# Row 1's attention interleaved earlier with chunk 0's products, and three small reorderings, in a fused windowed-attention and squared-ReLU kernel

## The chip, the cores and the metric

The kernel runs on one core of one Trainium2 chip. A core has five engines that run beside one another and meet through semaphores: TensorE (PE, matmuls and transposes; its weight loads are shown as PEld), VectorE (DVE), ScalarE (ACT), GpSimd (POOL) and SyncE (SP, which here only issues DMAs). The metric is the device time of one execution in microseconds (us), lower is better.

## The reference

Eight batch rows of 576 tokens, each with eight heads of 64 features, go through causal attention. Heads 0 to 3 see the last 32 tokens (sliding), heads 4 to 7 every fourth of the last 128 (dilated). The heads are then laid side by side as 4608 tokens of 512 features and go through two dense products with a squared ReLU between them.

```python
mask_plain = (rel >= 0) & (rel < window)
mask_dil = (rel >= 0) & (rel < window * dilation) & (rel % dilation == 0)
scores = np.where(masks[None, :, :, :], scale * q @ k.T, -1000000000.0)
attn = softmax(scores)
x = (attn @ v).transpose(0, 2, 1, 3).reshape(B * S, H * D)      # 4608 x 512
h = x @ w_in                                                    # 512 -> 2048
g = np.maximum(h, 0.0) ** 2
out = g @ w_out                                                 # 2048 -> 512
```

## The kernel before, in words

Attention works by batch row (0 to 7, 576 tokens), the dense part by chunk (0 to 8, 512 tokens). Since chunk c spans parts of rows c-1 and c, rows run ahead of chunks: while row b is in attention, the dense steps of an earlier chunk (chunk b-1) fill TensorE.

The order is written by hand. Every engine runs its own instructions in the order in which the program emits them. The dense part is a Python generator, and `pump(n)` (L520) emits its next n steps; a step is two matmuls of 128x512 (or four of 128x256). A call of `pump` between two pieces of attention puts dense work between them on TensorE, and with it the ScalarE and VectorE work of those steps on their queues.

A row of attention has these pieces. Rows 0 and 1 turn q and k by TensorE (`t_sliding` L538, `t_dilated` L556); VectorE and ScalarE copy the result to QKTp and QKTd. From row 2 on, VectorE puts the loaded q and k (tile ns) in token order (`by_token` L118, tile nr), SP writes nr to DRAM (dp) and reads it back through transposing DMAs (L229, L233). `attn_scores` (L712) makes four groups of scores, exponentials on ScalarE and masks on VectorE (tile AT). `attn_values` (L728) makes seven groups of values: three sliding (pav), four dilated (paw). After each, VectorE takes a reciprocal and a product (`normalize`, L622), and TensorE turns the result (px, py) for ScalarE to copy into xT, the dense part's input. The scores, values and, in row 1, the transposes share a PSUM pool of two buffers (`papool`).

`mm1_gen` (L318) is a chunk's first product: 16 groups of four matmuls into ph, each followed by a ReLU on ScalarE (rt) and a square on VectorE (g). Chunk 0's second product is `mm2_by_rows_gen` (L488): 32 steps, the first 24 of which leave nothing; its last eight finish the output tiles po of tokens 0 to 127, 128 to 255, and so on, and `store` (L466) copies each to ot on ScalarE. From chunk 2 on, the second product is done by seven half-size products (`mm2_strassen_gen`, L359), whose operands are sums and differences of parts of g (tile gs, `sum_of_g` L335).

Row 1 (L846 to L861): `pump(1000)` emits the whole first product of chunk 0, `pump(3)` six matmuls of its second product, then come the transposes with `pump(2)` after each, the scores with `pump(2)`, and the values with `pump(1)` (two after the first pav). In the middle of the values, after paw of the first dilated group, `then` puts row 2's `by_token` copy on VectorE and its two stores on SP. On SP these stores are followed by the output of chunk 0's first half (L462, after `store` of its second tile), the four transposing DMAs of row 2, the output of the second half, and the v loads of row 2. Row 2's q and k (ns) are loaded from the POOL queue (L822, which emits L112), behind `cast_sliding_v(1)` and the last quarter of w_out.

At the end (L933 to L937), chunk 7's generator is pumped for 20 steps, then ScalarE copies the second half of row 7's dilated values into xT (L695, called through `second_half`), then chunk 7 is finished and chunk 8 follows. The last half product ends in one add of 128x512 (L444) and one 256 KB DMA (L445).

Of the kernel before, what the change touches and what calls it, by code (L numbers as in the profile page):

```python
# [13 lines left out]
P = 128  # L14
# [3 lines left out]
def kernel(  # L18
# [9 lines left out]
    nc = tc.nc  # L28
# [11 lines left out]
    TOKC = 512  # L40
# [40 lines left out]
    HM = DM // 2  # L81
    HF = NFF // 2
    HTOK = TOKC // 2
# [98 lines left out]
    def halo_sliding(b, mp):  # L182
        m0, m1 = max(1, 2 * mp), 2 * mp + 2
        nc.scalar.copy(
            vp[b % 2][0:PADP, m0:m1, :, 0:D], vp[b % 2][P - PADP : P, m0 - 1 : m1 - 1, :, 0:D]
        )
# [78 lines left out]
    for m, w, pad in (  # L265
# [5 lines left out]
            out=lo_[:, 0:w], in0=relf[:, 0:w], scalar1=-pad - 0.5, scalar2=None, op0=ALU.is_gt  # L271
        )
        nc.vector.tensor_scalar(
            out=hi_[:, 0:w], in0=relf[:, 0:w], scalar1=W - pad - 0.5, scalar2=None, op0=ALU.is_lt
# [6 lines left out]
    for r in range(2):  # L281
        nc.vector.tensor_scalar(
            out=vd[r][:, 0, :, :, D],
# [12 lines left out]
    def mm1_half(c, ffc, ph, dmks, parts=None):  # L296
        lo = c * TOKC % XW
        cut = min(TOKC, XW - lo)
        parts = parts or [(0, cut, lo)] + ([(cut, TOKC, 0)] if cut < TOKC else [])
        for dmk in dmks:  # L300
            for t0, t1, x0 in parts:
                nc.tensor.matmul(  # L302
                    ph[:, t0:t1],
                    wi4[ffc // 4][:, dmk, :, ffc % 4],
                    xT[:, dmk, x0 : x0 + t1 - t0],
                    start=(dmk == 0 and t0 == 0),
                    stop=(dmk == NDM - 1),
                    skip_group_check=parts != [(0, TOKC, lo)],
                )
# [3 lines left out]
    def mm1_begin(c, ffc, parts=None):  # L313
        ph = pmool.tile([P, TOKC], FP32, name=f"ph{c}_{ffc}", tag="pm")
        mm1_half(c, ffc, ph, (0, 1), parts)
        return ph

    def mm1_gen(c, g, sums=False, begun=()):  # L318
        for ffc in range(NFF):
            if ffc < len(begun):  # L320
                ph = begun[ffc]
            else:
                ph = mm1_begin(c, ffc)
                yield
            mm1_half(c, ffc, ph, (2, 3), [(T0, TOKC, T0)] if begun and ffc < len(begun) else None)
            rt = osb.tile([P, TOKC], FP16, name=f"rt{c}_{ffc}", tag="rt")
            nc.scalar.activation(rt, ph[:], ACTF.Relu)  # L327
            nc.vector.tensor_mul(g[:, ffc, :], rt, rt)  # L328
            if c == 1 and ffc % 2 == 0:
                next(w_sums)  # L330
            if sums and ffc % 4 == 3 and ffc >= HF:
                sum_of_g(g, ffc - 3, ffc + 1)
            yield

    def sum_of_g(g, f0, f1):  # L335
        k = slice(f0 - HF, f1 - HF)
        nc.vector.tensor_add(gs[0][:, k], g[:, k, HTOK:], g[:, f0:f1, HTOK:])
        nc.vector.tensor_sub(gs[1][:, k], gs[0][:, k], g[:, k, 0:HTOK])
# [20 lines left out]
    def mm2_strassen_gen(c, g):  # L359
        A, Bk, Ck = "abc"  # L360
        banks = {}

        def wq(r, q):
            return lambda k: wo[2 * r + k // 4][:, k % 4, HM * q : HM * (q + 1)]

        def gq(i, r):
            return lambda k, t: g[:, HF * r + k, HTOK * i + P * t : HTOK * i + P * (t + 1)]

        def tq(n):
            return lambda k: wt[n][:, k]  # L370

        def sq(n):
            return lambda k, t: gs[n][:, k, P * t : P * (t + 1)]

        def product(bank, a, b, ts=(0, 1)):
            new = bank not in banks
            if new:
                banks[bank] = pmool.tile([P, 2, HM], FP32, name=f"p{bank}{c}", tag="pm")
            for t in ts:
                for k in range(HF):  # L380
                    nc.tensor.matmul(  # L381
                        banks[bank][:, t],
                        a(k, t),
                        b(k),
                        start=(new and t == 0 and k == 0),
                        stop=(k == HF - 1),
                        skip_group_check=True,
                    )
                    if k % 4 == 3 and (t, k) != (ts[-1], HF - 1):
                        yield  # L390

        def half(i):
            return otp.tile([P, 2, DM], FP32, name=f"o{i}_{c}", tag="ot")

        def take(o, j):
            ot = o[:, :, HM * j : HM * (j + 1)]
            nc.scalar.copy(ot, banks[A])  # L397
            return ot

        def leave(o, i, js):  # L400
            t0 = c * TOKC + HTOK * i
            m = slice(HM * js[0], HM * (js[-1] + 1))
            nc.sync.dma_start(
                out=out[t0 : t0 + HTOK, m].rearrange("(t p) m -> p t m", p=P), in_=o[:, :, m]
            )

        def add(ot, bank):
            nc.vector.tensor_add(ot, banks[bank], ot)  # L408

        last = c == NTOKC - 1  # L410

        nc.vector.tensor_sub(g[:, 0:HF, HTOK:], g[:, 0:HF, 0:HTOK], g[:, 0:HF, HTOK:])
        yield from product(A, gq(0, 0), wq(0, 0))
        upper = half("u")
        o11 = take(upper, 0)
        yield
        yield from product(Ck, gq(0, 1), wq(1, 0))
        add(o11, Ck)
        if last:
            leave(upper, 0, (0,))  # L420
        yield
        yield from product(A, sq(1), tq(1))
        lower = half("v")
        o21 = take(lower, 0)
        nc.vector.tensor_sub(gs[1], g[:, HF:, 0:HTOK], gs[1])
        yield
        yield from product(Bk, gq(1, 0), tq(2), (0,))
        yield
        yield from product(A, sq(0), tq(0))
        o22 = take(lower, 1)  # L430
        yield
        yield from product(Bk, gq(1, 0), tq(2), (1,))
        add(o22, Bk)
        if last:
            leave(lower, 1, (1,))
        yield
        yield from product(A, sq(1), wq(1, 1))
        take(upper, 1)
        leave(upper, 0, (1,) if last else (0, 1))
        while at_end:  # L440
            at_end.pop()()
        yield
        yield from product(Bk, gq(1, 1), tq(3))
        add(o21, Bk)  # L444
        leave(lower, 1, (0,) if last else (0, 1))  # L445
        yield

    def mm2(c, g, po, t, ffc):
# [71 lines left out]
    def pump(n):  # L520
        for _ in range(n):
            while pending:
                try:
                    next(pending[0])
                    break
                except StopIteration:
                    pending.pop(0)
# [184 lines left out]
    def attn_scores(b, gap, less=0, hooks={}):  # L712
        for hp in range(2):
            s_sliding(b, hp)
            if hp in hooks:
                hooks[hp]()
            pump(gap)
        for g in range(2):
            if g and b == 1:
                halo_sliding(b, 0)  # L720
            s_dilated(b, g)
            if 2 + g in hooks:
                hooks[2 + g]()
            if g and b == 2:
                halo_sliding(b, 0)
            pump(gap - less)

    def attn_values(b, gap, wide=False, then=None):  # L728
        xs = x_tiles(b)
        for mp in range(3):  # L730
            av_sliding(b, mp, xs)
            if b < 3:
                if mp < 2:
                    halo_sliding(b, mp + 1)
                else:
                    halo_dilated(b, 0)
            if then and b > 1 and mp == 4 - b:
                then()
            pump(gap + (b == 1 and mp == 0))
        x_sliding(b, 0, xs, wide)  # L740
        if b < 3:
            halo_dilated(b, 2)
        pump(gap)
        av_dilated(b, 0, 0, xs)
        if then and b == 1:
            then()
        pump(gap)
        x_sliding(b, 1, xs, wide)
        pump(gap)
        av_dilated(b, 0, 1, xs)  # L750
        pump(gap)
        for a in range(2):
            av_dilated(b, 1, a, xs)
            pump(gap)
        x_dilated(b, 0, xs, wide)
        pump(gap)
        x_dilated(b, 1, xs, wide)
# [87 lines left out]

    g0 = hidden(0)  # L846
    pending.append(mm1_gen(0, g0, False, begun))
    pump(1000)
    pending.append(mm2_by_rows_gen(0, g0))
    pump(3)  # L850
    n, m = nsd[1]
    for hp in range(2):
        t_sliding(1, n, hp, True)
# [1 line left out]
    for a in range(2):  # L855
        t_dilated(1, m, a, True)
        pump(2)
    attn_scores(1, 2)
    dp = []
    attn_values(1, 1, True, lambda: dp.append(keep_sliding_qk(2, by_token(2, ns))))  # L860
    pump(1000)  # L861
    transpose_sliding(2, dp[0])
# [68 lines left out]
        attn_values_by_dma(b, (copied, load_and_turn, cast, load_rest))  # L931
        pump(1000)
    pending.append(moe_gen(B - 1))  # L933
    pump(20)
    second_half.pop()()
    pending.append(moe_gen(B))
    pump(10000)  # L937
# [30 lines left out]
```

## Time and profile before

| what | us |
|---|---|
| median of five runs | 304.70 |
| lowest and highest run | 303.52, 305.51 |
| the profiled execution | 304.63 |
| its span, from first to last record | 302.5 |
| TensorE busy in the span | 286.6 |
| VectorE busy | 213.0 |
| ScalarE busy | 172.8 |
| GpSimd busy | 67.6 |

The span is what the profile's views cover; 2.1 us of the execution lie around it. Times in the views count from the start of the span. In a timeline each line is one run of like instructions: start, busy time, engine, line of the kernel, operation, output<-input, shapes, how many, and in brackets how long the engine sat idle before it and what released it. Busy times of neighbouring matmul groups overlap by a pipeline tail of some 0.1 to 0.2 us, so that starts, not busy times, are to be subtracted. In the list of DMA issues the last number is the time from issue to landing.

### The profile page before, as it was taken

The numbers are of one execution on the slowest core, as the hardware profiler recorded it, in microseconds if no ns is written. First come the engines' busy times: TensorE is split into PE (matmuls) and PEld (weight loads), VectorE is DVE, ScalarE is ACT, GpSimd is POOL, SyncE is SP. The second block draws the span as 40 slices with busy tenths as digits, with TensorE's granted clock in tenths as the row PEclk, the third lists the DMA queues.
The fourth block names the chain that finished last, engine by engine and source line by source line (L and its number), as shares of the span: only waits on it lengthen the run. The fifth ranks groups of instructions, "written<-read, shape, count | busy, mean of one in ns | idle before, by whom it ended". The sixth has DMA issues, their size and how long they took to land.

```text
span 302.5 us, 6903 instructions
## 1 busy us (share of the span) xinstructions
PE 286.6 (95%) x2768; PEld 193.6 (64%) x2768; DVE 213.0 (70%) x439; ACT 172.8 (57%) x293; POOL 67.6 (22%) x112
## 2 busy tenths in 40 slices
PE   0989999999999999999999999999999998999994
PEld 0556554555554569756889996568656964785583
DVE  7685459668843899499849984998599734824651
ACT  1866748679744952595348554855485547426620
POOL 4463009002702600540035023502230000000000
PEclk9999999999999999999999999999999999999999
DMA  7899996999499989998999799999972230003013
GB/s 113 169 211 215 203 196 110 215 219 225 116 186 170 250 145 190 223 261 134 170 188 266 157 145 192 217 233 157 171 210 41 41 139 0 2 10 132 0 36 106
DMA packets 77376, 46.61 MB, mean 154 GB/s; under 512 B 58400, under 2 KB 69152, under 8 KB 77344
## 3 DMA queue, kind: packets, MB, share of 16 engines
q1 hardware_dynamic: 68592, 32.54, 50.4%
q0 software_dynamic: 8752, 13.63, 26.6%
q8 instruction: 22, 0.36, 0.5%
q14 instruction: 10, 0.08, 0.1%
HBM read 36.70 MB, written 16.52 MB: 176 GB/s over the span
## 4 chain that ended last, share of the span: by engine, by line
PE 86%; DVE 5%; DMA 4%; ACT 2%; issue 1%; POOL 0%; SPq 0%; POOLq 0%
PE ph L302 38%; PE pa L381 16%; PE pb L381 8%; PE po L449 8%; PE pc L381 4%; PE paw L658 3%; DMA nd<-in_q_dram 3%; DVE AT L574 2%; PE pav L642 2%; PE ps L587 2%; PE pz L612 2%; PE pf L515 2%; DMA QKTp<-dp 1%; PE pd L561 1%; DVE g L328 1%
## 5 line engine op out<-in xcount | busy, mean ns | idle before, releaser
L302 PE MATMUL ph<-xT,wi 128*128 128x512 f16 (+2 forms) x648 | 134.6, 356 | 1.1 <-ACT xT L695 1.0
L327 ACT ACTIVATE rt<-ph 128x512 f16<-128x512 f32 x144 | 85.7, 609 | 45.6 <-PE ph L302 42.8
L302 PEld LDWEIGHTS <-wi 128*128 128x128 f16 x648 | 68.8, 114 | 46.0 <-issue 1.3
L328 DVE TENSOR_TENSOR g<-rt 128x512 f16<-128x512 f16 x144 | 63.4, 454 | 36.2 <-ACT rt L327 35.0
L381 PEld LDWEIGHTS <-g 128*128 128x128 f16 x448 | 43.2, 98 | 6.2 <-DVE g L328 0.2
L381 PEld LDWEIGHTS <-gs 128*128 128x128 f16 x336 | 32.5, 98 | 3.7
L449 PE MATMUL po<-wo,g 128*128 128x512 f16 x128 | 33.1, 379 | 0.0
L169 POOL CAST vp<-sv 128x512 f16<-128x512 f32 x24 | 15.4, 672 | 58.4 <-DMA sv<-in_v_dram 45.9
L381 PE MATMUL pb<-wt,g 128*128 128x256 f16 x224 | 27.9, 273 | 0.0
L408 DVE TENSOR_TENSOR ov<-pb,ov 128x512 f32<-128x512 f32 x14 | 9.7, 691 | 25.3 <-PE pb L381 20.0
L381 PE MATMUL pa<-wt,gs 128*128 128x256 f16 x224 | 27.1, 273 | 0.0
L177 POOL CAST vd<-sd 128x512 f16<-128x512 f32 (+1 forms) x32 | 22.0, 716 | 15.0 <-DMA sd<-in_v_dram 14.4
L397 ACT COPY ov<-pa 128x512 f32<-128x512 f32 x14 | 8.2, 586 | 26.7 <-PE pa L381 26.7
L630 DVE TENSOR_TENSOR xd<-paw,rcp_d 80x512 f16<-80x512 f32 (+1 forms) x32 | 21.9, 685 | 1.1
L571 ACT ACTIVATE AT<-pz 128x576 f16<-128x576 f32 x32 | 19.8, 692 | 1.3 <-PE pz L612 1.1
L574 DVE TENSOR_TENSOR AT<-AT,maskd 128x576 f16<-128x576 f16 x32 | 19.4, 636 | 1.6 <-ACT AT L571 1.1
L571 ACT ACTIVATE AT<-ps 128x576 f16<-128x576 f32 x32 | 19.2, 657 | 2.0 <-PE ps L587 1.5
L574 DVE TENSOR_TENSOR AT<-AT,maskp 128x576 f16<-128x576 f16 x32 | 16.1, 518 | 5.5 <-ACT AT L571 4.2
L397 ACT COPY ou<-pa 128x512 f32<-128x512 f32 x14 | 8.2, 586 | 19.2 <-PE pa L381 19.2
L630 DVE TENSOR_TENSOR xs<-pav,rcp_p 96x512 f16<-96x512 f32 x24 | 16.5, 686 | 0.8
L449 PEld LDWEIGHTS <-g 128*128 128x128 f16 x128 | 10.4, 98 | 8.3
L658 PEld LDWEIGHTS <-AT 128*128 128x128 f16 x256 | 11.9, 98 | 5.4 <-PE px L671 1.0
(81 smaller groups left out, 280.0 us busy)
## 6 DMA issues: line engine op xcount, KB each, us to landing
sv<-in_v_dram SPq DMA_DIRECT2D x14, 288.0 KB, 5.4
dp<-nr SPq DMA_DIRECT2D x12, 288.0 KB, 3.9
out_dram<-ou SPq DMA_DIRECT2D x6, 512.0 KB, 4.9
out_dram<-ov SPq DMA_DIRECT2D x6, 512.0 KB, 5.6
sd<-in_v_dram SPq DMA_DIRECT2D x8, 320.0 KB, 4.9
ns<-in_k_dram POOLq DMA_DIRECT2D x8, 288.0 KB, 6.7
ns<-in_q_dram POOLq DMA_DIRECT2D x8, 288.0 KB, 8.4
sd<-in_v_dram SPq DMA_DIRECT2D x8, 256.0 KB, 5.6
```

The costliest lines, as they stand in the source:

```text
L169: nc.gpsimd.tensor_copy(vp[b % 2][:, m : m + 2, :, 0:D], sv[:, :, m : m + 2, :].rearrange("p h m d -> p m h d"))
L177: nc.gpsimd.tensor_copy(vd[b % 2][p0:P, t, c : c + 2, :, 0:D], sd[p0:P, t, :, D * c : D * (c + 2)].rearrange("p h (c d) -> p c h d", d=D),)
L302: nc.tensor.matmul(ph[:, t0:t1], wi4[ffc // 4][:, dmk, :, ffc % 4], xT[:, dmk, x0 : x0 + t1 - t0], start=(dmk == 0 and t0 == 0), stop=(dmk ...
L327: nc.scalar.activation(rt, ph[:], ACTF.Relu)
L328: nc.vector.tensor_mul(g[:, ffc, :], rt, rt)
L381: nc.tensor.matmul(banks[bank][:, t], a(k, t), b(k), start=(new and t == 0 and k == 0), stop=(k == HF - 1), skip_group_check=True,)
L397: nc.scalar.copy(ot, banks[A])
L449: nc.tensor.matmul(po, g[:, ffc, t * P : (t + 1) * P], wo[ffc // 4][:, ffc % 4, :], start=(ffc == 0), stop=(ffc == NFF - 1),)
L571: nc.scalar.activation(AT[:, u, 0:UW], ps[:, :, 0 : UW // 2], ACTF.Exp, scale=scale)
L574: nc.vector.tensor_mul(AT[:, u, 0:UW], AT[:, u, 0:UW], mask)
L630: nc.vector.tensor_tensor(out=x, in0=pv, in1=rb, op=ALU.mult)
L658: nc.tensor.matmul(pav[:, e, h * (D + 2) : h * (D + 2) + D + 1], AT[:, 4 + h, off : off + P], vd[b % 2][:, t, 2 * a + e, h, 0 : D + 1], st ...
```

## The change

There are four parts. Row 1: chunk 0's first product is emitted only up to its fourteenth of 16 groups before row 1's transposes; the other two groups go between the transposes; the `pump(3)` is gone, one step is added behind the scores, and two more go behind the first pav and one more behind the second. Chunk 2: the first `sum_of_g` comes after group 12, not after group 11 (other chunks keep their order). Chunk 7: 44 steps instead of 20 come before the copy of `second_half`. Chunk 8: the last add and the last output DMA are split in two halves of 128x256, the second issued from ScalarE's queue.

```diff
@@ mm1_gen
-            if sums and ffc % 4 == 3 and ffc >= HF:
-                sum_of_g(g, ffc - 3, ffc + 1)
+            if sums and ffc == (12 if c == 2 else 11):
+                sum_of_g(g, 8, 12)
+            if sums and ffc == 15:
+                sum_of_g(g, 12, 16)
@@ mm2_strassen_gen
         yield from product(Bk, gq(1, 1), tq(3))
-        add(o21, Bk)
-        leave(lower, 1, (0,) if last else (0, 1))
+        if last:
+            for t, eng in enumerate((nc.sync, nc.scalar)):
+                o = o21[:, t]
+                nc.vector.tensor_add(o, banks[Bk][:, t], o)
+                t0 = c * TOKC + HTOK + P * t
+                eng.dma_start(out=out[t0 : t0 + P, 0:HM], in_=o)
+        else:
+            add(o21, Bk)
+            leave(lower, 1, (0, 1))
         yield
@@ attn_values
-            pump(gap + (b == 1 and mp == 0))
+            pump(gap + (b == 1 and 2 - mp))
@@ row 1
     pending.append(mm1_gen(0, g0, False, begun))
-    pump(1000)
+    pump(26)
     pending.append(mm2_by_rows_gen(0, g0))
-    pump(3)
     n, m = nsd[1]
...
     attn_scores(1, 2)
+    pump(1)
     dp = []
     attn_values(1, 1, True, lambda: dp.append(keep_sliding_qk(2, by_token(2, ns))))
     pump(1000)
@@ the end
     pending.append(moe_gen(B - 1))
-    pump(20)
+    pump(44)
     second_half.pop()()
```

## The prediction

> **What bounds the kernel now.** I read the page first, then the chain of waits, then timelines of the four places that the diff touches, then the DMA issues. Page and chain:
>
> ```profile
> PE 286.6 (95%) x2768; PEld 193.6 (64%) x2768; DVE 213.0 (70%) x439; ACT 172.8 (57%) x293; POOL 67.6 (22%) x112
> PE 86%; DVE 5%; DMA 4%; ACT 2%; issue 1%; POOL 0%; SPq 0%; POOLq 0%
> ```
>
> TensorE is the bound. Of its 15.9 us without work, 11 lie before row 0's dilated transposes (start 11.08) and 4.2 behind its last matmul (298.3). No instruction is added to it, so only idle stretches can be won or lost; there are about 0.5 to 1 us at each of three places. Row 1, timelines of TensorE and VectorE:
>
> ```profile
> 52.74 0.41 PE L642 MATMUL pav<-vp,AT 128*128 128x65 f16 x8 [0.50 <-DVE rcp_p L625]
> 59.03 0.41 PE L689 MATMUL py<-ident,xd 64*128 64x64 f16 x8
> 59.37 1.04 PE L449 MATMUL po<-wo,g 128*128 128x512 f16 x4
> 60.24 2.11 PE L302 MATMUL ph<-xT,wi 128*128 128x512 f16 x9
> ...
> 55.10 0.69 DVE L630 TENSOR_TENSOR xd<-paw,rcp_d 80x512 f16<-80x512 f32 x1
> 55.71 0.75 DVE L120 COPY nr<-ns 128x2304 f16<-128x2304 f16 x1
> 58.29 0.68 DVE L630 TENSOR_TENSOR xd<-paw,rcp_d 64x512 f16<-64x512 f32 x1
> ```
>
> The third pav waits for a PSUM buffer; after the last transposes (py) there are four po matmuls, then chunk 1. VectorE is without a gap from nr (55.71) to its last xd (ends 58.97), and py starts 0.06 behind that. What nr reads is loaded from the POOL queue; its timeline, and DMA issues of that stretch:
>
> ```profile
> 48.61 0.64 POOL L112 DMA_DIRECT2D ns<-in_q_dram  x1
> ...
> ns<-in_q_dram POOLq DMA_DIRECT2D x1, 288.0 KB, 6.7
> ```
>
> So q of row 2 lands at 48.61 + 6.7 = 55.3, and nr starts 0.4 later. That slack is hidden in the timeline, since VectorE was busy up to then. The other places:
>
> ```profile
> 110.33 0.42 PE L642 MATMUL pav<-vp,AT 128*128 128x65 f16 x8 [0.60 <-DVE xs L630]
> ...
> 254.27 1.06 ACT L695 COPY xT<-yd 128x512 f16<-128x512 f16 x1
> 255.37 4.69 PE L302 MATMUL ph<-xT,wi 128*128 128x512 f16 x21 [0.99 <-ACT xT L695]
> ...
> 298.37 0.69 DVE L408 TENSOR_TENSOR ov<-pb,ov 128x512 f32<-128x512 f32 x1 [2.75 <-PE pb L381]
> 299.09 0.37 SPq L403 DMA_DIRECT2D out_dram<-ov  x1
> ```
>
> Chunk 2 waits 0.60 for VectorE, chunk 7 0.99 for a ScalarE copy, and the end is an add and a DMA.
>
> [...] shows SP's issues in program order. [...]
>
> **Row 1, front.** Chunk 0's last two groups start at 37.93 - 8 x 0.216 = 36.20, against 39.15 for the transposes before. They now start there, but their loads were issued at 22.76 (q) and 23.90 (nd, q) and took 13.7 and 15.6 us, landing at 36.5 and 39.5. So the first waits 0.3. The PSUM pool has two buffers, and each set of transposes needs the copies of the set before. Those copies (0.64 and 0.76, then 0.74 and 0.82) now have a ReLU (0.60) and a square (0.43) between them on both engines. I take 0.3 lost at the second set, 0.1 at the third, and 0.6 at the fourth, whose buffer comes free only after ReLU 15, its square (40.8) and the QKTd copy (41.6). With no stall the scores would start at 36.20 + 4 x 0.48 + 16 x 0.216 = 41.6; with these at 43.0, against 44.78. Bounds: 41.9 (the landing alone) and 44.8.
>
> **Row 1, values.** From first scores to first reciprocal VectorE took 6.9 us (44.78 to 51.68), so now that is 49.9. Behind the last scores and the first two pavs there are now 3, 3 and 2 steps of 0.43 (2, 2 and 1 before). The first pav came 5.5 after the first scores, now 5.9; with 0.26 for a pav, TensorE reaches the third at 43.0 + 5.9 + 1.6 + 1.1 = 51.6, long after its buffer is free (50.8): the 0.50 stall is gone, and about 0.4 of small ones after it. The first paw comes at 53.0, its xd is done by 54.3, and next in VectorE's queue is nr. Before, that was at 55.71 and its data was there. Now it must wait for q of row 2, whose POOL queue follows v's loads and not TensorE: POOL starts the casts in front of it at 45.28, after 17.1 us of waiting for v. So nr starts at 55.4 whether the scores began at 41.9 or at 44.0. Behind it on VectorE are three reciprocals and products; the fourth paw and both py wait for the PSUM buffers that these free. They stay dense, so py starts at 59.03 - 0.31 = 58.72. Behind py there are now 12 po matmuls, not 4: the six steps left of 32 (26 are pumped before). Chunk 1 starts at 58.72 + 0.34 + 12 x 0.216 = 61.65, against 60.24: **+1.4 us**. Low end, if the load did not bind: from first scores to chunk 1 TensorE's own work is 60.24 - 44.78 - 1.4 (its stalls, summed from the starts) + 14 x 0.216 = 17.1, so chunk 1 could come at 41.9 + 17.1 + 0.5 for stalls that stay = 59.5, -0.7. High end: scores at 44.8 give another 0.7, +2.1.
>
> **SP behind row 1.** The second tile's `store` now comes 0.9 behind py, near 60.1 to 60.7, where it was at 57.51. The output DMA waits for it on SP with row 2's four transposing DMAs behind: they start near 61.2 instead of 59.83, +1.35, and the v loads with them. TensorE is +1.4 later too, and row 2's first scores had 3.8 us between the landing of QKTp (66.05 by the semaphore records) and use (69.83), so I charge nothing. Row 2's v casts end at 77.7 and their first use is ScalarE's halo copy at 78.03, a slack of 0.35 that a larger shift of SP alone would break.
>
> **Chunk 2.** The first reciprocal and product now pass ahead of two gs operations (0.69 each), so the third pav no longer waits 0.60. But VectorE is dense from 107.15 to 120, and the second product still ends at 111.69; px, which needs it, moves from 111.89 to 111.80. **-0.1**, bounds 0 and -0.6.
>
> **Chunk 7.** The 0.99 wait goes. The copy (1.06) now falls behind the third half product, where ScalarE is idle for 2 us between copies and no matmul needs xT. Its DMA landed before 254.27. **-1.0**, bounds -0.9 and -1.0.
>
> **Chunk 8.** The second add has no wait of its own in the program, so the first one waits for all matmuls: the adds still start at 298.37[...]. Each DMA carries 128 KB; from 512 KB (2.8) and 256 KB (2.2) I take 0.3 less. The first goes 0.3 earlier, the second 0.1 later: **-0.2**, bounds -0.5 and +0.2 (ScalarE's queue is unused for DMA in this trace).
>
> Sum: 304.63 + 1.4 - 0.1 - 1.0 - 0.2 = 304.7, equal to the median of the runs, 304.70.
>
> **Rivals.**
> 1. The early start is kept (faster): the load lands over 1 us sooner, and the copies between the transposes cost nothing. Row 1 then gives -0.7, in all 304.63 - 0.7 - 0.1 - 1.0 - 0.2 = 302.6. For it: the stalls at 52.74 and behind it are real. Against it: the 0.4 us of slack, and two engines with a ReLU and a square more between copies.
> 2. The SP queue takes over (slower): the late output of chunk 0 holds the transposes and, behind them, v of row 2. The DMA engines are full there (share 1.08 from 60.2 to 69.8), and POOL waited 4.41 us for this load. Decisive is a landing over 1.4 + 0.35 later. At twice the 1.35 of SP's delay the values of row 2 wait 0.95, and with row 3's scores, which already wait 0.6 on the transposes at 97.70, another 0.6: 304.7 + 1.55 = 306.3.
> 3. Row 1 ends even (the load does not bind, the front costs its 1.3: 43.0 + 17.1 + 0.2 = 60.3): 303.3, from the other three parts.
>
> **Numbers.** Changes under 0.5% (1.5 us) can't be told from none here. Forecast 304.7 with its own range 303.6 to 305.8: 0.52; rival 1: 0.13; rival 2: 0.21; rival 3: 0.14. Rival 1 and a third of rival 3 count as faster, rival 2 and the forecast's highest ends as slower: faster 0.18, same 0.58, slower 0.24. The range from 302.5 to 306.3 leaves out half of each outer case, 0.17.
>
> **What would show it.** In the profile after: a wait of VectorE at nr for the DMA of ns, about 1 us; nr near 55.4; 12 po matmuls between py and chunk 1, which starts near 61.6; no idle time at the third pav of row 1; a wait at px in chunk 2; no 0.99 wait in chunk 7; two adds and DMAs at the end. A start of chunk 1 below 60 proves the forecast wrong, as does an idle TensorE at row 2's values.

## The result, and the profile after

| | kernel before | changed kernel |
|---|---|---|
| median of the runs on record | 304.7 us (48 runs) | 304.4 us (27 runs) |
| ratio | | 0.999, 95% interval 0.9975 to 1.0005 |
| profiled execution | 304.63 us, span 302.5 | 302.9 us, span 300.9 |

No change that can be told from none. The ratios here and below leave out the executions that the record marks as slow, and they are not the quotients of the medians; where the two tell different things, both are given. The profiled execution of the changed kernel is one of its quick ones, 1.5 us under its median, so the two spans differ by more than the medians do, and the profile has to be read stretch by stretch. The first lines of the page after:

```profile
span 300.9 us, 6906 instructions
PE 286.2 (95%) x2768; PEld 193.7 (64%) x2768; DVE 210.9 (70%) x440; ACT 172.9 (57%) x293; POOL 67.2 (22%) x112
PE 79%; DMA 15%; POOL 2%; DVE 1%; SPq 1%; issue 1%; ACT 0%; DVEq 0%; POOLq 0%
```

The work is the same, and the share of DMAs on the chain of waits went from 4% to 15%: that chain now runs through the v load for which POOL waits (16.6 us) and then through row 2's q (7.0). Row 1 in the timelines of TensorE (from the fourth dilated values to chunk 1) and VectorE, after:

```profile
56.95 0.41 PE L667 MATMUL paw<-vd,AT 128*128 128x65 f16 x8 [1.55 <-DVE rcp_d L634]
58.53 0.40 PE L698 MATMUL py<-ident,xd 64*128 64x64 f16 x8
58.86 2.76 PE L458 MATMUL po<-wo,g 128*128 128x512 f16 x12
61.46 2.75 PE L302 MATMUL ph<-xT,wi 128*128 128x512 f16 x12
```

```profile
55.21 0.76 DVE L120 COPY nr<-ns 128x2304 f16<-128x2304 f16 x1 [1.50 <-DMA ns<-in_q_dram]
```

VectorE waits 1.50 us for row 2's q; TensorE waits 1.55 us for VectorE's work behind that; then 12 po matmuls come where there were four, and chunk 1 begins at 61.46 instead of 60.24. The wait at the third pav (0.50) is gone. The wait at px in chunk 2 that the prediction named as a sign does not show. Chunk 7 and the end, after:

```profile
249.84 7.50 PE L302 MATMUL ph<-xT,wi 128*128 128x512 f16 x34
...
264.13 0.58 ACT L399 COPY ov<-pa 128x512 f32<-128x512 f32 x1 [2.91 <-PE pa L383]
264.61 1.10 ACT L704 COPY xT<-yd 128x512 f16<-128x512 f16 x1
...
297.15 0.76 DVE L449 TENSOR_TENSOR ov<-pb,ov 128x256 f32<-128x256 f32 x2 [2.74 <-PE pb L383]
297.61 0.35 SPq L451 DMA_DIRECT2D out_dram<-ov  x1
298.00 0.37 ACTq L451 DMA_DIRECT2D out_dram<-ov  x1
```

The DMA issues of the end, after (size, and us from issue to landing):

```profile
out_dram<-ov SPq DMA_DIRECT2D x1, 128.0 KB, 1.7
out_dram<-ov ACTq DMA_DIRECT2D x1, 128.0 KB, 1.8
```

Chunk 7's first product runs through, and ScalarE's copy lies where ScalarE had been idle for 2.91 us. 128 KB land in 1.7 and 1.8 us, 256 KB had taken 2.2.

### The profile page after: what moved, and what is told of

It is laid out like the page before. It is cut to its first block, busy times and chain, and to the rows that moved or that the text cites. A ratio compares the mean times of both kernels' runs of the same rounds, so it can differ in the third digit from the quotient of the medians.

```text
span 300.9 us, 6906 instructions
## 1 busy us (share of the span) xinstructions
PE 286.2 (95%) x2768; PEld 193.7 (64%) x2768; DVE 210.9 (70%) x440; ACT 172.9 (57%) x293; POOL 67.2 (22%) x112
## 4 chain that ended last, share of the span: by engine, by line
PE 79%; DMA 15%; POOL 2%; DVE 1%; SPq 1%; issue 1%; ACT 0%; DVEq 0%; POOLq 0%
PE ph L302 38%; PE pa L383 16%; PE pb L383 8%; DMA sv<-in_v_dram 6%; PE po L458 6%; DMA wi<-in_moe_w_in_dram 4%; PE pc L383 4%; DMA ns<-in_q_dram 4%; PE paw L667 2%; PE pav L651 1%; PE pz L621 1%; PE ps L596 1%; POOL vp L169 1%; PE py L698 1%; SPq L129 1%
## 5 line engine op out<-in xcount | busy, mean ns | idle before, releaser
L328 DVE TENSOR_TENSOR g<-rt 128x512 f16<-128x512 f16 x144 | 62.2, 445 | 37.8 <-ACT rt L327 36.7
L410 DVE TENSOR_TENSOR ov<-pb,ov 128x512 f32<-128x512 f32 x13 | 9.0, 691 | 23.2 <-PE pb L383 17.9
L399 ACT COPY ov<-pa 128x512 f32<-128x512 f32 x14 | 8.2, 585 | 25.7 <-PE pa L383 22.5
L583 DVE TENSOR_TENSOR AT<-AT,maskd 128x576 f16<-128x576 f16 x32 | 18.6, 607 | 1.4 <-ACT AT L580 0.9
```

Source lines behind the costliest of these rows:

```text
L583: nc.vector.tensor_mul(AT[:, u, 0:UW], AT[:, u, 0:UW], mask)
```

## The experiments

My theory: row 1's new order costs some 1.4 us, since nr waits for a load whatever TensorE does and eight more matmuls lie behind that wait; the three other parts pay for it. The rivals: row 1 gains and something else loses; or SP's queue is what holds row 1.

A measure that does not depend on how quickly the kernel's start went in a given execution, as long as nr does not wait, is the time from the end of the 14th group of chunk 0's first product to the first matmul of chunk 1. In the new order that end is the start of row 1's first transposes; in the old order it is that start less 2.95 us (39.15 - 36.20 in the profile of before; with matmul starts throughout, the stretches of the old order would be 0.16 longer and those of the new order 0.09). Call it the row 1 stretch. Where nr waits, chunk 1 follows the landing of the load instead, and an early start makes the stretch longer: no_row1, the longest of the old order, has the earliest 14th group of the six (35.1). There the time from nr's start to chunk 1 says more: it is 4.5 us in all six profiles with the old order, and 6.25 in the changed kernel, after_again and row1_only_again. From the profiles of all kernels:

| kernel | row 1 | load of row 2's q | wait at nr | row 1 stretch | ratio to before, 95% interval |
|---|---|---|---|---|---|
| before | old | late | 0 | 24.0 | |
| chunk2_only | old | late | 0 | 24.0 | 1.0002 (0.9979 to 1.0025) |
| chunk7_only | old | late | 1.19 | 25.2 | 0.9934 (0.9909 to 0.9959) |
| no_row1 | old | late | 1.92 | 26.0 | 0.993 (0.9903 to 0.9958) |
| before_q_early | old | early | 0 | 23.4 | 0.9978 (0.996 to 0.9997) |
| three_q_early | old | early | 0 | 24.0 | 0.992 (0.989 to 0.995) |
| changed kernel | new | late | 1.50 | 25.6 | 0.999 (0.9975 to 1.0005) |
| after_again | new | late | 1.60 | 25.7 | one execution |
| row1_only | new | late | 1.94 | 27.8 | 1.0052 (1.0031 to 1.0072) |
| row1_only_again | new | late | 0.55 | 27.5 | one execution |
| row1_q_early | new | early | 0 | 24.3 | 0.9917 (0.9888 to 0.9946) |
| row1_nr_late | new, nr last | late | 0 | 24.6 | 0.9948 (0.9926 to 0.997) |
| row1_covered | new, 4 steps moved | late | 1.25 | 23.9 | 0.9942 (0.9919 to 0.9965) |
| row1_even_early | new, 4 steps spread | early | 0 | 24.9 | 0.9935 (0.9902 to 0.9968) |

**Row 1's part alone.** The kernel before with these lines:

```diff
-    pump(1000)
+    pump(26)
     pending.append(mm2_by_rows_gen(0, g0))
-    pump(3)
...
     attn_scores(1, 2)
+    pump(1)
...
-            pump(gap + (b == 1 and mp == 0))
+            pump(gap + (b == 1 and 2 - mp))
```

The last line gives three steps instead of two behind the first pav and two instead of one behind the second.

> The kernel before with the change's row 1 part alone. My theory (the load of row 2's q holds nr, and 12 po matmuls lie behind the last transposes): chunk 1 starts 1.2 to 1.6 us later than before, nr shows a wait of about 1.5 us for the DMA of ns, and the time is 305.5 to 306.2, +0.8 to +1.5 (the 0.6 us that row 3's scores waited before may be given back on the way). Rival (the early start is kept): 303.8 to 304.2, and no wait at nr.

305.91 us against 304.25 of the kernel before, run beside it, ratio 1.0052: +1.6 us with an interval from +0.9 to +2.2, a little over the +1.5 of my range. The rival, 304.2 or less and no wait at nr, falls. From VectorE's and TensorE's timelines:

```profile
55.90 0.76 DVE L120 COPY nr<-ns 128x2304 f16<-128x2304 f16 x1 [1.94 <-DMA ns<-in_q_dram]
...
63.61 2.75 PE L302 MATMUL ph<-xT,wi 128*128 128x512 f16 x12
```

Chunk 1 starts 3.4 us later than in the profile of before, not the expected 1.2 to 1.6. Of this 1.5 us goes with a granted clock of 0.50 behind the wait (last section). Seven of the 19 executions have a mean granted clock of 0.994 or less, by which I count such stretches; the median of the other twelve is 305.60, or +1.35.

**The three other parts alone.** The changed kernel with those lines undone.

> The changed kernel with row 1 as before: chunk 2, chunk 7 and chunk 8 parts alone. Mine: 303.2 to 303.6, 1.1 to 1.5 us under the kernel before, so faster than the whole change by about 1 us. Rival (row 1 pays for itself): no faster than the whole change, 304.2 to 304.8.

302.61 us, ratio 0.993: -2.1 us (interval -2.9 to -1.3; the medians, 304.25 and 302.61, give -1.6). So the whole change is a gain of some 2 us with a loss of 1.6 to 1.8 us on top. The direction is as I expected, and the gain is larger. This profile also showed what the single profile of before had not, VectorE's timeline with row 1 in its old order:

```profile
56.56 0.76 DVE L120 COPY nr<-ns 128x2304 f16<-128x2304 f16 x1 [1.92 <-DMA ns<-in_q_dram]
```

In the old order, too, nr waits for the load in some executions (here and in chunk7_only, 1.19 us).

**The load earlier.** The changed kernel with:

```diff
     load_v(1)
+    ns = load_sliding_qk(2)
     cast_sliding_v(1)
     load_w_out((3,))
-    ns = load_sliding_qk(2)
```

> The changed kernel with the load of row 2's sliding q and k issued ahead of row 1's v casts on the POOL queue, nothing else. Mine: it lands some 6 us sooner, nr waits for nothing, chunk 1 starts near 59.9 in place of 61.5, and if the load was all that held row 1, the time falls to 302.7 to 303.3. Rival (SP's queue, held by the output of chunk 0's first half, takes the place of the load): the wait at nr goes, but row 2's values or row 3's scores wait instead and the time stays at 304.0 to 304.6.

302.61 us, ratio 0.9917, 2.5 us under before by the ratio and 1.6 by the medians. The POOL queue issues the loads at 39.78 and 40.40 instead of near 48, and nr waits for nothing:

```profile
40.40 0.63 POOL L112 DMA_DIRECT2D ns<-in_q_dram  x1
...
55.11 0.75 DVE L120 COPY nr<-ns 128x2304 f16<-128x2304 f16 x1
```

The row 1 stretch falls from 25.6 to 24.3. Chunk 1 started at 61.37, not at 59.9, because in this execution the 14th group ended 1.3 us later than in the profile of the changed kernel (37.09 against 35.82). The rival with SP's queue falls: no wait appeared at row 2's or row 3's attention.

The same edit in the kernel before, and in the kernel with the three other parts:

> The kernel before with row 2's sliding q and k loaded ahead of row 1's v casts, nothing else. If the load holds nr in the old order too (two profiled runs in which row 1 had the old order showed waits of 1.2 and 1.9 us at nr), chunk 1 starts 24.0 to 24.4 us after the 14th group of chunk 0's first product in place of 24.0 to 26.0, and the time falls by 0.5 to 1.5 us, to 0.995 to 0.998 of the kernel before. Rival (the old order has the load in time as a rule): 0.999 to 1.001.

> The three other parts of the change, row 1 in the old order, and the early load. If both gains add up: 301.2 to 302.2, 0.989 to 0.992 of the kernel before, the fastest of all. Rival (row 1's new order is worth something once the load is early): no faster than the changed kernel with the early load, 0.9917.

Before: 0.9978, a small gain whose interval just excludes none at all (it ends at 0.9997), with a stretch of 23.4, less than the 24.0 to 24.4 expected. With the three parts: 302.54 us, 0.992, as fast as the best but not clear of no_row1 (0.993). That the gains add up is thus not shown. Nor does row 1's new order show a gain with the load out of its way: one profile of it has a stretch of 24.3, two of the old order have 23.4 and 24.0, and the ratios are 0.9917 and 0.992.

**nr out of the way.** The changed kernel with row 2's copy and its stores emitted last:

```diff
         av_dilated(b, 0, 0, xs)
-        if then and b == 1:
-            then()
         pump(gap)
...
         for a in range(2):
             av_dilated(b, 1, a, xs)
+            if a and then and b == 1:
+                then()
             pump(gap)
```

> The changed kernel with row 2's nr copy and its stores behind row 1's last values on VectorE, instead of behind the first dilated ones; the load stays where it was. If what costs time is that nr blocks the products behind it on VectorE: no wait of TensorE at the fourth dilated values, chunk 1 starts 24.2 to 24.8 us after the 14th group, and the time is 0.992 to 0.995 of the kernel before. Rival (row 2's transposes, now 2 us later, take its place): TensorE waits at row 2's scores and the time is 0.998 to 1.002.

303.26 us, ratio 0.9948; TensorE no longer waits among row 1's values, and the stretch is 24.6, of which 0.38 and 0.53 are waits of the first transposes for row 1's own loads. Both theories had a part: TensorE's timeline at row 3's scores shows a wait that most of the other profiles don't have:

```profile
98.00 0.43 PE L596 MATMUL ps<-QKTp 64*128 64x96 f16 x12 [1.23 <-DMA QKTp<-dp]
```

The rival named row 2's scores, which did not wait. What delayed row 3's transposes here stays open.

**The eight matmuls in front of the wait.** The changed kernel with four more steps behind the third dilated values:

```diff
         for a in range(2):
             av_dilated(b, 1, a, xs)
-            pump(gap)
+            pump(gap + (4 if b == 1 and a == 0 else 0))
```

> The changed kernel with four more steps (8 po matmuls) behind the third dilated values of row 1, so that 4 po matmuls lie behind the last transposes instead of 12; the load and nr stay. If the cost of row 1 is those 8 matmuls lying behind a wait that they could have filled: TensorE's wait at the fourth dilated values goes, chunk 1 starts 23.8 to 24.4 us after the 14th group instead of 25.6, and the time is 302.3 to 303.0, 0.991 to 0.995 of the kernel before. Rival (the front of row 1, the copies between the transposes, is what costs): at least 25.2 us and 0.997 or more.

TensorE's and VectorE's timelines of this kernel:

```profile
54.69 2.32 PE L458 MATMUL po<-wo,g 128*128 128x512 f16 x10
56.85 0.42 PE L667 MATMUL paw<-vd,AT 128*128 128x65 f16 x8
58.69 1.04 PE L458 MATMUL po<-wo,g 128*128 128x512 f16 x4
59.56 2.75 PE L302 MATMUL ph<-xT,wi 128*128 128x512 f16 x12
```

```profile
54.85 0.76 DVE L120 COPY nr<-ns 128x2304 f16<-128x2304 f16 x1 [1.25 <-DMA ns<-in_q_dram]
```

VectorE waits for the load as before, but TensorE works through it, on ten po matmuls from 54.69 to 56.85, and four are left behind py. The stretch is 23.9, in the range of the theory; 302.47 us, ratio 0.9942. This is the cleanest of the tests, since the load, nr and the front of row 1 are all as in the changed kernel: the cost was the place of the eight matmuls, with the 1.5 us that came on top in row1_only, where a granted clock of 0.50 followed the wait (last section).

**The four steps spread, with the early load.** One step more behind the first, second and third dilated values and the second px, with the early load.

> The changed kernel with the early load and the four steps spread over the four gaps behind the first, second and third dilated values and the second px. If VectorE's seven reciprocals and products are then all that is left: chunk 1 starts 23.3 to 23.8 us after the 14th group and the time is 0.988 to 0.991 of the kernel before, the fastest of all. Rival (VectorE bounds it whatever TensorE has to do): 24.2 us as with the early load alone, 0.9917.

302.57 us, 0.9935: no faster than the others, where I had expected the fastest. In its profile the first transposes waited 1.05 and 0.48 us for row 1's own q, k and dilated loads; less these, the stretch of 24.9 would be 23.4. It doesn't tell the two theories apart.

**Chunk 7 alone and chunk 2 alone.** The kernel before with `pump(44)` for `pump(20)`, and the kernel before with the later first `sum_of_g`:

> The kernel before with the 44 steps ahead of chunk 7's ScalarE copy alone. Mine: the 0.99 us wait of TensorE goes, 303.6 to 303.9. Rival (the wait moves to the half products behind it): 304.5 to 304.9.

> The kernel before with the later first sum of g in chunk 2 alone. Mine before the result: 0.1 us, 0.999 to 1.001. Rival (what the two traces suggest): row 3's first scores to the first px take 13.4 us in place of 14.2, 0.7 us less, 0.997 to 0.998 of the kernel before.

Chunk 7: 302.91 us, 0.9934, more than expected: even the near end of its interval is -1.25 us, though the medians (304.25 and 302.91) give -1.3. In the profiles chunk 7 lasts 27.2 us in each of the five with the old place of the copy and 26.04 in each of the nine with the new one, so the part is worth 1.15 by the traces. What else the ratio holds stays open. Chunk 2: 1.0002, no gain. Its TensorE timeline shows why:

```profile
110.42 1.04 PE L383 MATMUL pa<-wo,g 128*128 128x256 f16 x8
111.29 0.34 PE L673 MATMUL px<-ident,xs 96*128 96x96 f16 x4
111.88 0.26 PE L673 MATMUL px<-ident,xs 96*128 96x96 f16 x2 [0.25 <-DVE xs L632]
```

The third pav no longer waits, px begins sooner, and then its last two transposes, the only ones that read the second product, wait for VectorE. The rival read px's first start, which falls from 14.2 to 13.4 us behind row 3's scores (13.42 here), and took it for the gain. From these scores to the start of chunk 3 it is 27.6 to 28.1 us in the five profiles without the part (27.8 in before) and 27.2 to 27.7 in the nine with it (27.7 here), on average 0.4 less; the one profile of this part alone has 0.16 less than before.

**Two kernels once more.**

> The changed kernel once more. The wait at nr follows the landing of row 2's q, so chunk 1 starts 6.25 us behind nr's start again, whatever the front of the kernel took.

> Row 1's part alone once more, for the granted clock. If one idle stretch of 2 us sets TensorE to half speed whenever it falls so: half speed for 3.4 us behind it again if the wait is 2 us or more, none if it is shorter.

In the first, nr starts at 55.90 and chunk 1 at 62.15, 6.25 behind, as in the changed kernel (55.21 and 61.46). The second missed its expectation, and belongs to the last section.

## Why the prediction was right

The total, 304.7 for 304.4, was right, and so was the step that decided: nr bound to the load, with eight matmuls behind it. The sizes were less so. Row 1's loss was taken too small by some 0.2 us and the gain of the three other parts by 0.3 (medians) to 0.8 (ratio). That these errors have opposite signs and offset each other in part is luck.

- **nr and the load.** Predicted: nr near 55.4, a wait of about 1 us, chunk 1 near 61.65. Measured: 55.21, 1.50 and 61.46. That the 0.4 us of slack in front of nr would not be enough was the step that decided, and row1_q_early, row1_nr_late and row1_covered, each of which removes another link, all take the loss away.
- **The size of row 1.** Predicted +1.4, measured +1.6 alone (0.9 to 2.2). The term took 0.31 off because nr in the profile of before started 0.31 later than its data allowed. In other executions of the old order nr waits for the load itself (1.19 and 1.92 us); then nr starts at the landing in either order, and the difference is the whole of 8 matmuls of 0.216 (12 of them took 2.60, from 58.86 to 61.46), 1.7, the 6.25 less 4.5 us from nr to chunk 1. One profile showed the slack of one execution. The other part of the miss is TensorE's clock, which the prediction did not have: without the seven executions whose mean granted clock is 0.994 or less, the medians give +1.35. The runs don't separate the two.
- **The idle time.** The prediction puts 11 of TensorE's 15.9 us without work ahead of 11.08. By the windows view TensorE works 3.65 us there, so 7.4 lie ahead of it, 4.2 behind the last matmul and 4.3 between. No term of the sum rests on this count.
- **The front.** Predicted: 1.3 us lost at row 1's transposes, scores 6.8 us after the 14th group. Measured: 6.4 (35.82 to 42.22). As forecast, it had no bearing on chunk 1, since the load came later.
- **SP behind row 1.** Predicted start of row 2's transposing DMAs near 61.2 and no wait at row 2. Measured 61.08, with the output DMA ahead of them on SP at 60.55, and no wait.
- **Chunk 7.** Predicted -1.0 with bounds -0.9 and -1.0, by the traces -1.15. The view's 0.99 counts from the end of the matmuls' pipeline tail; by starts, 249.69 + 21 x 0.216 = 254.22 to 255.37, TensorE stood for 1.15.
- **Chunk 8.** Predicted -0.2. From the last add's start to the end of the span it is 4.1 us in the kernels with one add and 3.75 to 3.9 in those with two, -0.38 between the two profiles. The mis-sized term is the DMA, where I took 0.3 off for the smaller size and it was 0.4 to 0.5 (1.7 and 1.8 against 2.2). That the first DMA would go 0.3 earlier and the second 0.1 later was an estimate of mine that the trace of before did not show. Measured, both adds take 0.76 where one had taken 0.69, and the DMAs are issued 0.46 and 0.85 behind the start of the adds, against 0.72 for the one DMA (299.09 - 298.37).
- **Chunk 2.** Predicted -0.1, timed at none; the traces give -0.4 on average. The working had all of px behind the second product, but four of its six transposes read only the first.

The three parts sum to some -1.9 by the traces and to -2.1 by the ratio or -1.6 by the medians, where the sum had -1.3.

## What to carry to other kernels

A buffer wait that vanished in one place (0.50 us at the third pav) was worth nothing here, since the queue behind it was held by a load (1.50 us at nr); look at how long before its use each input lands, not only at the waits that the profile shows. Work that can fill a wait has to be emitted in front of it: the eight matmuls cost nothing in front of the fourth dilated values and 1.7 us behind the last transposes. Where the slack is a few tenths, one profile doesn't say whether it is there in the other executions: 0.4 us in before, none in chunk7_only and no_row1, where nr waited 1.19 and 1.92. A wait of TensorE can cost more than its own length: in row1_only one of 1.99 us cost 1.5 more, with a granted clock of 0.50 behind it. The mean granted clock of each execution suggests how often that happened, there in 7 of 19.

## What the runs showed of the hardware

In two of the 14 profiles the page's line of TensorE's granted clock has one slice of 0.7 (row1_only from 53 to 61 us, row1_only_again from 38 to 46), in the others every slice is 0.9 or more. In row1_only the windows view gives 0.59 from 57.6 to 58.5, 0.50 from there to 61.0 and 0.92 from 61.0 to 62.0, which comes to some 3.4 us at 0.50; in row1_only_again it gives 0.50 from 39.0 to 42.3 and 1.00 up to 39.0 and from 42.4 on. (Behind the last matmul it is below 1 as well: 0.89 on average from 298.0 to 302.5 in before, 0.81 from 297.2 to 300.9 in the changed kernel.) In row1_only the stretch came behind a wait of 1.99 us at the fourth dilated values; in row1_only_again behind a wait of 1.62 us of the first transposes for row 1's own q. Two answers of the windows view (stretch, its length, busy time and count of PE, PEld, DVE, ACT and POOL, then the granted clock, the DMA share and GB/s), the first from row1_only, the second from row1_only_again:

```profile
55.00:57.60 2.60, 0.64 (x9) 0.15 (x5) 1.67 (x4) 0.00 (x0) 0.00 (x0) 1.00 1.04 163
58.50:59.50 1.00, 1.00 (x11) 0.72 (x10) 0.65 (x1) 0.00 (x0) 0.00 (x0) 0.50 1.03 274
62.00:64.00 2.00, 2.00 (x11) 0.92 (x9) 0.00 (x0) 1.37 (x3) 0.00 (x0) 1.00 0.18 68
```

```profile
35.50:37.40 1.90, 0.25 (x6) 0.14 (x9) 0.44 (x2) 0.42 (x1) 0.00 (x0) 1.00 1.09 214
40.00:42.30 2.30, 2.30 (x13) 1.37 (x12) 1.07 (x3) 0.78 (x3) 0.00 (x0) 0.50 1.28 210
42.40:44.00 1.60, 1.60 (x16) 1.01 (x15) 1.07 (x2) 0.75 (x2) 0.00 (x0) 1.00 1.07 172
```

TensorE's timeline of row1_only, at the wait:

```profile
57.64 0.54 PE L658 MATMUL paw<-vd,AT 128*128 128x65 f16 x8 [1.99 <-DVE rcp_d L625]
57.98 1.04 PE L449 MATMUL po<-wo,g 128*128 128x512 f16 x2
58.82 0.74 PE L689 MATMUL py<-ident,xd 80*128 80x80 f16 x8
```

Two po matmuls take 0.84 us in that stretch (57.98 to 58.82) instead of 0.43, and the time from nr to chunk 1 is 7.7 us instead of 6.25: with the clock at 0.50 behind it the wait costs 1.5 us more than its own length. This is why both row 1 stretches of that kernel stand apart in the table; in row1_only_again the wait of 1.62 us itself lies in the stretch, too.

How often it happened can be estimated from the mean granted clock that the record has for each execution: one such stretch takes 3.4 x 0.5 / 303 = 0.006 off it. The values form two groups, 0.994 and less (both profiles with the stretch are in it) and 0.996 and more (all the others), with none between. Only the two profiles show the stretch itself; that the other executions of the lower group had one is my reading of their mean clock.

| kernels | executions with 0.994 or less |
|---|---|
| row1_only | 7 of 19 |
| changed kernel, with the profiled execution | 6 of 28 |
| row1_q_early | 1 of 6 |
| new order, wait at the fourth dilated values gone (row1_nr_late, row1_covered, row1_even_early) | 0 of 46 |
| kernel before, as run beside the experiments | 4 of 103 |
| other kernels with the old order | 0 of 59 |

In row1_only the medians of the two groups are 307.5 and 305.6, in the changed kernel 305.1 and 303.9. By this count half speed belongs to what row 1's new order costs with the late load: taken over all executions, some 0.2 us of the changed kernel's mean (304.34 against 304.10 without them) and 0.8 of row1_only's (306.32 against 305.53).

The length of the wait alone does not sort the profiles. Waits of 1.99 us at the fourth dilated values (row1_only) and 1.62 us at the first transposes (row1_only_again) had a granted clock of 0.50 behind them. Waits at the fourth dilated values of 1.94 us in no_row1 (1.00 from 56.0 to 62.0) and of 1.66 in after_again (no slice of its page below 0.9) did not. What decides stays open.
